# Seven-product tiles of a float32 attention and cosine feed-forward kernel: outputs in one run, the last product put off

## The chip, the cores and the metric

The kernel runs on one core of a Trainium2 chip. The metric is the device time of the whole program in microseconds (us). A core has TensorE (PE: matmuls; PEld is its loading of weights), VectorE (DVE), ScalarE (ACT), GpSimd (POOL) and SyncE (SP, whose queue issues the DMAs). Each engine works through its own instructions in the order of the program and waits for the others by semaphores.

## The reference

Chunked attention (64 positions to a chunk, 64 to a head) makes the 4608 x 512 matrix x, and a feed-forward layer with a cosine follows. All of it is float32.

```python
scores = scale * np.matmul(q_c, k_c.transpose(0, 1, 2, 4, 3))
scores = scores - np.max(scores, axis=-1, keepdims=True)
attn = np.exp(scores)
attn = attn / (np.sum(attn, axis=-1, keepdims=True) + 1e-09)
out = np.matmul(attn, v_c)
...
x = out.transpose(0, 2, 1, 3).reshape(B * S, H * D)   # 4608 x 512
h = x @ w_in                                          # 512 x 2048
g = h * np.cos(h)
return g @ w_out                                      # 2048 x 512
```

## The kernel before, in words

**Tiles.** The 4608 tokens are nine tiles of 512 (TOK). The 2048 hidden features are 16 chunks of 128 (fc), or eight pairs of chunks (k). Every float32 operand is split into a high part and a low rest, and a float32 product is three matmuls: high by high, high by low, low by high. Tiles 0 and 1 do the hidden layer directly (`hidden`, line 559). Tiles 2 to 8 do it by seven block products to a pair in place of eight (`pair`, line 804): A11, S3, S2, A12, A22, S1 and S4, each six matmuls of 256 columns, with sums of blocks of w_in that were made once, kept in HBM, and are streamed back two products at a time (`load_two`, line 733) into eight rooms in SBUF.

**A pair.** Two PSUM banks hold four halves: a and d in bank1, b and c in bank2. A11 goes to a, S3 to d. ScalarE copies a to b and d to the SBUF tile ds (line 839). S2 is added onto b, ScalarE copies b to c, A12 is added onto a, A22 onto c, S1 and at last S4 onto b. VectorE adds ds to c and b (`add`, line 842), which makes h2, the hidden values of the pair's second chunk; a and the final b are the two halves of the first chunk's.

**The cosine.** For each chunk g = h cos(h) is made in steps: `whole` (ScalarE, line 848: the number of turns as an integer), `turn` (VectorE, line 851: h less whole turns), `sine` (ScalarE, line 855), `times` (VectorE, line 858). The first chunk does this in halves of 256 columns, the second in one of 512. `high` (ScalarE, line 866, or VectorE, line 864, where exponentials stand in the queue) rounds g to its high part, and `low` (VectorE, line 870) makes the rest. Both are put into the next pair by the list `pair_before`.

**Output.** Each chunk of g gives four output parts (`projected_by_parts`, line 594), each three matmuls of 512 columns onto one of four PSUM banks acc0 to acc3, which add over the 16 chunks of a tile. The parts wait in the queue `due_parts`; `go(n)` (line 792) takes n of them. The last part of a bank puts `finish` (line 619) on the list `full`: a copy of the bank to SBUF (line 236) and a store. `go` empties `full` ahead of each part it takes. The next tile's first part begins anew in the same bank.

**Order.** From tile 2 on the order of every engine's instructions is written out by hand, and `kept` (line 224) holds it. A pair places its output parts at four points with the tuple `after`, normally (3, 0, 2, 3): three between S3 and S2, two between S1 and S4, three after S4. Where one tile's last parts are due (pair 1, with exponentials in the queue) it is (4, 0, 2, 2), with the copies of `finish` right behind the four.

**Attention of the next tile** runs between: `run_of_short` (line 941) puts a burst of 64 x 64 matmuls ahead of pair 0 (scores) and behind pair 5 (LAST_TURN; weighted values), using the two h banks and the two a banks of PSUM. After pair 0 the exponentials go to `exponentials_due`, two ScalarE instructions that pair 1 takes; Exp and Sin need different tables, which ScalarE loads in between. The sums, quotients and transpositions go to VectorE in the list `soon`, some at each of four places of a pair (`slots`); the next tile's x blocks are made in pairs 6 and 7 (`ahead`, `soon`).

PSUM has eight banks here: four acc, two h, two a. In the kernel before every pair uses the two h banks.

Of the kernel before, what the change touches and what calls it, by code (L numbers as in the profile page):

```python
# [21 lines left out]
P = 128  # L22
# [3 lines left out]
LAG = 3  # L26

PAD = 32

SHIFT = 28  # L30

# [166 lines left out]
def attention_then_cos_ffn(ctx: ExitStack, tc, qT, kT, v, w_in, w_out, out, wide):  # L198
# [65 lines left out]
    for fc in range(NFC):  # L264
        for name, n in (("in", NCC * P), ("out", DM)):
            if wide:
                raw = wts.tile([P, 4 * n + 2 * PAD], U16, name=f"w_{name}{fc}")
            else:
                raw = wts.tile([P, 2 * n + PAD], F32, name=f"w_{name}{fc}")
            w_raw[name, fc] = (raw, n)  # L270

    def load_weight(name, fc):
# [8 lines left out]
    def split_weight(name, fc, low):  # L281


        raw, n = w_raw.pop((name, fc))
        made = []

        def w():
            if not made:
                made.append(dec.tile([P, n], F32, name="w"))
            return made[0]  # L290

        nothing = lambda: None
        if not wide:
            pieces = [lambda: nc.gpsimd.tensor_copy(w(), raw[:, :n])] + [nothing] * 2
        else:

            both = raw.bitcast(U32)[:, : 2 * n].rearrange("p (n k) -> p n k", k=2)  # L300
            lower, upper = both[:, :, 0], both[:, :, 1]

            def joined():
                bits = w().bitcast(U32)
                kept(nc.vector.scalar_tensor_tensor(
                    bits, bits, 3, low, op0=ALU.logical_shift_left, op1=ALU.bitwise_or
                ))

            pieces = [
                lambda: kept(nc.scalar.activation(  # L310
                    w(), upper.bitcast(F32), AF.Prelu, scale=2.0 ** -(MORE // 8), alpha=-(2.0**32))),
                lambda: kept(nc.scalar.activation(low, lower, AF.Copy, scale=LOWEST)),
                joined,
            ]

        def high(by):
            o = SHIFT if name == "in" else 0
            parts = wts.tile([P, 2 * n + PAD], F32R, name=f"w_{name}{fc}")
# [251 lines left out]
    def activated(t, fc, h):  # L570


        g = gp.tile([P, TOK], F32, name="g", bufs=2)
# [20 lines left out]
    def projected_by_parts(s, sums_out):  # L594

        t, fc = order[s]
        first = s == 0 or order[s - 1][0] != t
        last = s == len(order) - 1 or order[s + 1][0] != t

        def part(sub):  # L600
            g_hi, g_lo = g_parts[t, fc]
            w_hi, w_lo = w_parts["out", fc]
            if first:
                acc[sub] = bank("acc", sub)
            o = acc[sub]
            ss = slice(sub * P, (sub + 1) * P)
            matmul(o, g_hi[:, ss], w_hi, start=first, stop=False)
            matmul(o, g_hi[:, ss], w_lo, start=False, stop=False)
            matmul(o, g_lo[:, ss], w_hi, start=False, stop=last)
            if last:  # L610
                sums_out.append(lambda by=None, sub=sub, o=o: finish(t, sub, o, fc == NFC - 1, by))

        return [lambda sub=sub: part(sub) for sub in range(NSUB)]

# [182 lines left out]
    def g_room():  # L797
# [3 lines left out]
        room = w_in_room(G_ROOM, F32R)[:, PAD:]  # L801
        return room[:, :TOK], room[:, TOK : 2 * TOK]

    def pair(t, k):
# [14 lines left out]

        b, c = bank2[:, :HALF], bank2[:, HALF:]  # L820
# [3 lines left out]
        def product(out, j, begin=False):  # L824
# [4 lines left out]
            for cc in range(2):  # L829
# [11 lines left out]
        def add(out, in_):  # L841
            kept(nc.vector.tensor_tensor(out, in_, ds, op=ALU.add))  # L842

        g1, g2 = (gp.tile([P, TOK], F32, name="g", bufs=2) for _ in range(2))
        first, second = slice(0, HALF), slice(HALF, TOK)

        def whole(g, h):
            kept(nc.scalar.activation(g.bitcast(I32), h, AF.Identity, bias=0.25, scale=0.5 / math.pi))  # L848

        def turn(g, h):  # L850
            kept(nc.vector.scalar_tensor_tensor(  # L851
                g, g.bitcast(I32), -2.0 * math.pi, h, op0=ALU.mult, op1=ALU.add))

        def sine(g):
            kept(nc.scalar.activation(g, g, AF.Sin, bias=0.5 * math.pi))  # L855

        def times(g, h):
            kept(nc.vector.tensor_tensor(g, h, g, op=ALU.mult))  # L858

        def high(g, fc):  # L860
            hi, lo = g_parts[t, fc] = g_room()

            if exponentials_due:
                kept(nc.vector.tensor_copy(hi, g))
            else:
                kept(nc.scalar.copy(out=hi, in_=g))  # L866

        def low(g, fc):
            hi, lo = g_parts[t, fc]
            kept(nc.vector.tensor_tensor(lo, g, hi.bitcast(F32), op=ALU.subtract))  # L870

        if behind:
            slots = [0, 1, 1, 2]
        elif k < LAST_TURN:
            slots = [1, 1, 1, 8]
        elif k == LAST_TURN:
            slots = [max(len(soon) - 2, 0), 1, 1, 0]
        elif k == LAST_TURN + 1:  # L880
            slots = [0, 1, 0, 3]
        else:
            slots = [0, 1, 1, len(soon)]
        ahead = deque(pieces.pop("ahead", ()))

        product(a, A11, begin=True)
# [36 lines left out]
        whole(g1[:, second], b)  # L923
        take(ahead, 1)
        turn(g1[:, second], b)
        sine(g1[:, second])
        turn(g2, h2)
        times(g1[:, second], b)
        sine(g2)
        times(g2, h2)  # L930

        pair_before.extend([
            lambda: high(g1, 2 * k), lambda: low(g1, 2 * k),
            lambda: high(g2, 2 * k + 1), lambda: low(g2, 2 * k + 1),
        ])
        take(soon, slots[3])
        s0 = STAGE + (t - 2) * NFC + 2 * k
        for s in (s0, s0 + 1):
            due_parts.extend(projected_by_parts(s, full))

    def run_of_short(t, scored):

# [447 lines left out]
```

## Time and profile before

| what | value |
| --- | --- |
| median of 3 runs | 833.36 us (832.65 to 833.37) |
| the profiled execution: span from first to last instruction | 831.5 us |
| mean granted TensorE clock | 0.995 |
| ScalarE's waits for TensorE ahead of line 839 | 138.2 us, 93 times |
| ScalarE's waits for VectorE ahead of line 855 | 132.1 us, 162 times |
| HBM read and written | 148.90 and 25.17 MB |

The median lies 1.9 us above the span of the profiled execution. The chain of waits follows the work back from the last instruction, at each step to what released it. Waits of an engine that is not on that chain cost nothing by themselves. In a row of the profile stand the engine, the line of the kernel, the operation, out<-in by the names of tiles, the shape, and the count; in a timeline the first two numbers are the start and the length in us, and a bracket at the end is the idle time ahead of it and what ended it.

### The profile page before, as it was taken

To read this page: it belongs to the slowest core of one execution; us is meant where nothing else is said; L and a number is where in the kernel's file an instruction comes from. 1 tells how busy PE (TensorE), PEld (TensorE's weight loads), DVE (VectorE), ACT (ScalarE), POOL (GpSimd) and SP (SyncE) were. 2 spreads that over 40 slices of the span, in tenths; PEclk is the share of its full clock that TensorE was granted. 3 is DMA by queue.
4 is the path that set the end of the run, shared out by engine and by line. 5 is a ranking of instruction groups with operands and counts; after the bars stand their busy time and mean duration, and the time that the engine had idled before them with its cause. 6 is when DMAs were issued, how large, how long until landed. Compare 5 with 4: busy or idle time off the path is not lost.

```text
span 831.5 us, 17325 instructions
## 1 busy us (share of the span) xinstructions
PE 817.8 (98%) x6800; PEld 717.9 (86%) x6800; DVE 648.0 (78%) x1222; ACT 466.2 (56%) x955; POOL 133.2 (16%) x127
## 2 busy tenths in 40 slices
PE   6999999999999999999999999999999999999998
PEld 5778888888888889988998899898988899899996
DVE  5889888877889688967897879878896889665443
ACT  4999865454554645463645464565446454644443
POOL 2455577586410000000000000000000000000000
PEclk8999999999999999999999999999999999999999
DMA  9991606485695766575757585676657565456521
GB/s 336 417 395 69 229 30 224 146 291 196 202 337 173 254 197 233 178 259 180 272 177 231 177 279 177 213 239 209 207 176 254 197 232 177 157 178 226 178 75 51
DMA packets 70034, 175.21 MB, mean 211 GB/s; under 512 B 6976, under 2 KB 21312, under 8 KB 69952
## 3 DMA queue, kind: packets, MB, share of 16 engines
q1 hardware_dynamic: 69952, 174.09, 61.6%
q8 instruction: 54, 0.88, 0.4%
q14 instruction: 28, 0.23, 0.1%
HBM read 148.90 MB, written 25.17 MB: 209 GB/s over the span
## 4 chain that ended last, share of the span: by engine, by line
PE 91%; DMA 6%; ACT 1%; DVE 1%; SPq 0%; issue 0%; DVEq 0%; ACTq 0%
PE acc L232 46%; PE h L232 44%; DMA w_out<-in_w_out_dram 4%; PE a L232 1%; DMA kt<-in_kT_dram 1%; DMA vt<-in_v_dram 1%; SPq L229 0%; DVE g L851 0%; ACT L446 0%; ACT L582 0%; PE a L475 0%; ACT w L310 0%; ACT x L543 0%; ACT e L446 0%; ACT g L855 0%
## 5 line engine op out<-in xcount | busy, mean ns | idle before, releaser
L232 PE MATMUL acc<-w_out,g_hi 128*128 128x512 f32 x928 | 289.7, 393 | 0.0
L232 PE MATMUL h<-x,w_in 128*128 128x256 f32 (+1 forms) x1728 | 269.0, 304 | 0.0
L232 PEld LDWEIGHTS h<-x,w_in 128*128 128x128 f32 x1728 | 244.1, 188 | 25.5 <-ACT h L839 2.2
L232 PEld LDWEIGHTS acc<-w_out,g_hi 128*128 128x128 f32 x928 | 164.6, 188 | 28.6
L232 PE MATMUL acc<-w_out,g_lo 128*128 128x512 f32 x464 | 181.2, 390 | 0.0
L855 ACT ACTIVATE g<-g 128x256 f32<-128x256 f32 x168 | 82.3, 490 | 132.1 <-DVE g L851 132.1
L232 PE MATMUL h<-w_in,w_in 128*128 128x256 f32 x1008 | 138.3, 281 | 0.5 <-ACT h L839 0.5
L232 PEld LDWEIGHTS h<-w_in,w_in 128*128 128x128 f32 x1008 | 129.3, 188 | 7.1 <-DVE w_in L842 2.2
L839 ACT COPY h<-h 128x256 f32<-128x256 f32 x112 | 40.0, 357 | 139.6 <-PE h L232 138.2
L232 PEld LDWEIGHTS acc<-w_out,g_lo 128*128 128x128 f32 x464 | 87.1, 188 | 19.2
L232 PE MATMUL acc<-w_out,w_in 128*128 128x512 f32 x336 | 86.0, 393 | 0.0
L842 DVE TENSOR_TENSOR w_in<-h,w_in 128x256 f32<-128x256 f32 x112 | 42.3, 419 | 43.6 <-ACT x L238 22.4
L870 DVE TENSOR_TENSOR g_lo<-g,g_hi 128x512 fp32r<-128x512 f32 x84 | 57.4, 686 | 23.5 <-ACT g_hi L866 22.1
L232 PEld LDWEIGHTS acc<-w_out,w_in 128*128 128x128 f32 x336 | 59.6, 188 | 10.3
L496 DVE STREAM_TRANSPOSE pts<-e 32x256 f32<-32x256 f32 x128 | 55.6, 435 | 1.9
L858 DVE TENSOR_TENSOR g<-w_in,g 128x512 f32<-128x512 f32 x56 | 39.1, 698 | 20.4 <-ACT g L855 20.4
L851 DVE SCALAR_TENSOR_TENSOR g<-g,h 128x256 f32<-128x256 int32 x112 | 46.4, 414 | 9.8 <-ACT g L848 9.0
L858 DVE TENSOR_TENSOR g<-h,g 128x256 f32<-128x256 f32 x112 | 46.9, 419 | 8.0 <-ACT g L855 6.8
L848 ACT ACTIVATE g<-h 128x256 int32<-128x256 f32 x112 | 43.0, 384 | 8.2 <-PE h L232 4.2
L866 ACT CAST g_hi<-g 128x512 fp32r<-128x512 f32 x72 | 44.9, 623 | 0.0
L496 DVE STREAM_TRANSPOSE e<-e 32x256 f32<-32x256 f32 x96 | 41.8, 436 | 1.7
L851 DVE SCALAR_TENSOR_TENSOR g<-g,w_in 128x512 f32<-128x512 int32 x56 | 38.8, 693 | 0.0
(116 smaller groups left out, 907.1 us busy)
## 6 DMA issues: line engine op xcount, KB each, us to landing
w_in<-combo SPq DMA_DIRECT2D x196, 512.0 KB, 4.0
combo<-w_in SPq DMA_DIRECT2D x56, 256.0 KB, 3.2
qt<-in_qT_dram SPq DMA_DIRECT2D x36, 256.0 KB, 5.4
kt<-in_kT_dram SPq DMA_DIRECT2D x36, 256.0 KB, 5.5
w_in<-in_w_in_dram SPq DMA_DIRECT2D x16, 512.0 KB, 9.8
w_out<-in_w_out_dram SPq DMA_DIRECT2D x16, 512.0 KB, 9.9
vt<-in_v_dram SPq DMA_DIRECT2D x22, 256.0 KB, 4.8
qt<-in_v_dram SPq DMA_DIRECT2D x12, 256.0 KB, 4.6
```

The source lines that it names most:

```text
L232: kept(nc.tensor.matmul(*args, **kw))
L496: kept(nc.vector.transpose(out=dst[o : o + BL, :, qb], in_=src[i : i + BL, :, kb]))
L839: kept(nc.scalar.copy(out=out, in_=in_))
L842: kept(nc.vector.tensor_tensor(out, in_, ds, op=ALU.add))
L848: kept(nc.scalar.activation(g.bitcast(I32), h, AF.Identity, bias=0.25, scale=0.5 / math.pi))
L851: kept(nc.vector.scalar_tensor_tensor(g, g.bitcast(I32), -2.0 * math.pi, h, op0=ALU.mult, op1=ALU.add))
L855: kept(nc.scalar.activation(g, g, AF.Sin, bias=0.5 * math.pi))
L858: kept(nc.vector.tensor_tensor(g, h, g, op=ALU.mult))
L866: kept(nc.scalar.copy(out=hi, in_=g))
L870: kept(nc.vector.tensor_tensor(lo, g, hi.bitcast(F32), op=ALU.subtract))
```

## The change

Four things, in tiles 2 to 8:

- The seventh product, S4, with the second half of the first chunk (whole, turn, sine, times) and that chunk's high and low (the list `rest`), is put off into the next pair, where S4 stands between S3 and S2. A pair without a next one in line (`whole_now`: pair 5 and pair 7 ahead of a burst, and the very last) does them itself. high(1) and low(1), those of the second chunk, now stand at the pair's own end.
- The output parts are taken in one place, behind S1: eight parts, 24 matmuls. A pair with none before it (pairs 0 and 6 of a tile, behind a burst) takes two parts between S3 and S2 and two at the end; a `whole_now` pair takes five, then S4, then three.
- Odd pairs use the two a banks, even pairs the two h banks.
- The second chunk of a pair now comes first in the order of output parts (`fc ^ 1`). Both exponentials are taken together behind copy(c, b). `finish` has no place of its own in a pair any more; `go` alone empties `full`. A third buffer for g takes the room of the padding behind the w_out tiles. A streamed room is loaded again after the later of its two reads.

```diff
+SPARE = {"in": PAD, "out": 0}
...
-    order += [(t, fc) for t in range(NT) if t != 1 for fc in range(0 if t else GROUP, NFC)]
+    order += [(0, fc) for fc in range(GROUP, NFC)]
+    order += [(t, fc ^ 1) for t in range(FAST, NT) for fc in range(NFC)]
...
-        behind = bool(exponentials_due)
-        if behind:
-            after = (4, 0, 2, 2)
-        elif len(due_parts) < 12:
-            after = (1, 0, 2, 1)
-        elif t == NT - 1 and k == NPAIR - 1:
-            after = (2, 1, 2, 0)
+        behind = lean[0] = bool(exponentials_due)
+        last = t == NT - 1 and k == NPAIR - 1
+        whole_now = last or t + 1 < NT and k == LAST_TURN or t + 2 < NT and k == NPAIR - 1
+        before = waiting.pop() if waiting else None
+        if k % 2:
+            bank1, bank2 = bank("a", 0), bank("a", 1)
         else:
-            after = (3, 0, 2, 3)
-        bank1, bank2 = (ps_h.tile([P, TOK], F32, name="h") for _ in range(2))
+            bank1, bank2 = (ps_h.tile([P, TOK], F32, name="h") for _ in range(2))
...
-            if n % 2:
+            reads[n // 2] = reads.get(n // 2, 0) + 1
+            if reads[n // 2] == 2:
                 load_two(fc)
...
+        rest = [
+            lambda: (product(b, S4), whole(0, b, second), turn(0, b, second)),
+            lambda: sine(0, second),
+            lambda: times(0, b, second),
+            lambda: high(0),
+            lambda: low(0),
+        ]
...
         product(a, A11, begin=True)
         product(d, S3)
         take(ahead, 1)
         copy(b, a)
         copy(ds, d)
         take(ahead, 1)
-        if not behind:
-            take(pair_before, 2)
-        go(after[0])
-        take(full, len(full))
-        if behind:
-            take(pair_before, len(pair_before))
-        take(exponentials_due, 1)
+        if before:
+            then(0)
+        else:
+            go(2)
         product(b, S2)
         copy(c, b)
-        take(exponentials_due, 1)
-        take(pair_before, len(pair_before))
-        take(ahead, 1)
+        take(exponentials_due, len(exponentials_due))
         product(a, A12)
-        product(c, A22)
-        whole(g1[:, first], a)
         take(ahead, 1)
         take(soon, slots[0])
-        go(after[1])
+        then(1)
+        then(2)
+        product(c, A22)
         product(b, S1)
+        whole(0, a, first)
+        take(ahead, 1)
+        turn(0, a, first)
         add(h2[:, first], c)
         add(h2[:, second], b)
-        turn(g1[:, first], a)
+        sine(0, first)
+        times(0, a, first)
+        then(3)
+        whole(1, h2)
+        take(ahead, 1)
+        then(4)
+        turn(1, h2)
+        sine(1)
         take(pair_after, len(pair_after))
         take(soon, slots[1])
-        sine(g1[:, first])
-        times(g1[:, first], a)
+        times(1, h2)
+        if before:
+            n = 8 if len(due_parts) >= 12 else 4
+        else:
+            n = 2
+        if last:
+            n = 4
+        elif whole_now:
+            n = 5
+        go(n)
+        if whole_now:
+            rest[0]()
+            go(8 if last else 3)
+            rest[1]()
+            rest[2]()
+        high(1)
         take(soon, slots[2])
-        go(after[2])
-        whole(g2, h2)
-        product(b, S4)
-        go(after[3])
...
+        low(1)
         take(soon, slots[3])
+        if whole_now:
+            pair_before.extend(rest[3:])
+        else:
+            waiting.append(rest)
```

`then(i)` runs the i-th entry of the list that the pair before left, if there is one. `low(i)` puts the four output parts of its chunk into `due_parts`.

More of the change, by code (lines that the diff above doesn't have):

```diff
@@ L317, in high @@
             o = SHIFT if name == "in" else 0
-            parts = wts.tile([P, 2 * n + PAD], F32R, name=f"w_{name}{fc}")
+            parts = wts.tile([P, 2 * n + SPARE[name]], F32R, name=f"w_{name}{fc}")
             hi, lo = parts[:, o : o + n], parts[:, o + n : o + 2 * n]
@@ L570, in activated @@
     def activated(t, fc, h):
-        g = gp.tile([P, TOK], F32, name="g", bufs=2)
+        g = gp.tile([P, TOK], F32, name="g")
         n = g.bitcast(I32)
@@ L842, in add @@
             kept(nc.vector.tensor_tensor(out, in_, ds, op=ALU.add))
-        g1, g2 = (gp.tile([P, TOK], F32, name="g", bufs=2) for _ in range(2))
+        g = {}
         first, second = slice(0, HALF), slice(HALF, TOK)
[L847 to L864, printed above, removed]
-            else:
[L866 to L870, printed above, removed]
+        def whole(i, h, part=slice(0, TOK)):
+            if i not in g:
+                g[i] = gp.tile([P, TOK], F32, name="g")
+            kept(nc.scalar.activation(g[i][:, part].bitcast(I32), h, AF.Identity, bias=0.25, scale=0.5 / math.pi))
@@ new lines, in turn, with sine, times, high @@
+        def turn(i, h, part=slice(0, TOK)):
+            o = g[i][:, part]
+            kept(nc.vector.scalar_tensor_tensor(
+                o, o.bitcast(I32), -2.0 * math.pi, h, op0=ALU.mult, op1=ALU.add))
+        def sine(i, part=slice(0, TOK)):
+            o = g[i][:, part]
+            kept(nc.scalar.activation(o, o, AF.Sin, bias=0.5 * math.pi))
+        def times(i, h, part=slice(0, TOK)):
+            o = g[i][:, part]
+            kept(nc.vector.tensor_tensor(o, h, o, op=ALU.mult))
+        def high(i):
+            hi, lo = g_parts[t, 2 * k + i] = g_room()
+            if lean[0]:
+                kept(nc.vector.tensor_copy(hi, g[i]))
+            else:
+                kept(nc.scalar.copy(out=hi, in_=g[i]))
@@ new lines, in low @@
+        def low(i):
+            hi, lo = g_parts[t, 2 * k + i]
+            kept(nc.vector.tensor_tensor(lo, g[i], hi.bitcast(F32), op=ALU.subtract))
+            s = STAGE + (t - FAST) * NFC + 2 * k + 1 - i
+            due_parts.extend(projected_by_parts(s, full))
+        rest = [
[5 more added lines that the diff above has]
+        ]
@@ L874, in pair, with then @@
+        def then(i):
+            if before:
+                before[i]()
         if behind:
@@ L882, in pair @@
         else:
-            slots = [0, 1, 1, len(soon)]
+            slots = [1, 1, 1, len(soon)]
         ahead = deque(pieces.pop("ahead", ()))
@@ L914, in pair @@
+        take(ahead, 1)
+        then(4)
+        turn(1, h2)
+        sine(1)
         take(pair_after, len(pair_after))
         take(soon, slots[1])
-        sine(g1[:, first])
-        times(g1[:, first], a)
-        take(soon, slots[2])
-        go(after[2])
-        whole(g2, h2)
-        product(b, S4)
-        go(after[3])
[L923 to L935, printed above, removed]
+        times(1, h2)
+        if before:
+            n = 8 if len(due_parts) >= 12 else 4
[11 more added lines that the diff above has]
+            rest[2]()
```

16 lines of the change are left out of this document (8 added, 8 removed).

## The prediction

> **What bounds the kernel now.** I read the page first, then the chain of waits.
>
> ```profile
> span 831.5 us, 17325 instructions
> PE 817.8 (98%) x6800; PEld 717.9 (86%) x6800; DVE 648.0 (78%) x1222; ACT 466.2 (56%) x955; POOL 133.2 (16%) x127
> ...
> PEclk8999999999999999999999999999999999999999
> ...
> PE 91%; DMA 6%; ACT 1%; DVE 1%; SPq 0%; issue 0%; DVEq 0%; ACTq 0%
> ```
>
> TensorE is on 91% of the chain that ended last. Nothing else can give much; anything that makes TensorE wait is paid in full. The chain in order of time has start, length and count of each piece:
>
> ```profile
> 196.70 2.72 PE acc L232 x12
> ...
> 320.90 2.82 PE h L232 x24
> ...
> 329.28 2.08 PE acc L232 x9
> 331.36 2.82 PE h L232 x24
> ```
>
> A product matmul (256 columns) takes 2.82/24 = 0.1175 us, an output matmul in an undisturbed stretch 2.72/12 = 0.2267. Two like pieces one pair apart start 331.36 - 320.90 = 10.46 us apart. A pair has 42 products and 24 output matmuls: 42 x 0.1175 + 24 x 0.2267 = 4.94 + 5.44 = 10.38. So only 0.08 us of a pair is lost. The nine output matmuls behind products take 2.08 where 9 x 0.2267 = 2.04: each change from products to outputs costs some 0.04.
>
> The change reorders all engines, so I need the hand-overs. Timelines of TensorE, ScalarE and VectorE, one fence each:
>
> ```profile
> 441.87 1.57 PE L232 MATMUL h<-w_in,w_in 128*128 128x256 f32 x12
> ```
> ```profile
> 466.60 0.86 PE L232 MATMUL acc<-w_out,w_in 128*128 128x512 f32 x3
> ```
> ```profile
> 441.37 0.36 ACT L839 COPY h<-h 128x256 f32<-128x256 f32 x1 [1.61 <-PE h L232]
> ```
> ```profile
> 464.95 0.62 ACT L866 CAST g_hi<-g 128x512 fp32r<-128x512 f32 x1
> 465.47 0.39 ACT L848 ACTIVATE g<-h 128x256 int32<-128x256 f32 x1
> ...
> 470.38 0.63 ACT L855 ACTIVATE g<-g 128x512 f32<-128x512 f32 x1 [0.18 <-DVE g L851]
> ```
> ```profile
> 466.80 0.76 DVE L842 TENSOR_TENSOR w_in<-h,w_in 128x256 f32<-128x256 f32 x2 [0.50 <-PE h L232]
> ...
> 471.05 0.69 DVE L858 TENSOR_TENSOR g<-w_in,g 128x512 f32<-128x512 f32 x1 [0.36 <-ACT g L855]
> ```
>
> From product S1's end (466.60, the next matmul starts) to VectorE: 0.20. From ScalarE's end (471.01) to VectorE: 0.04. From ScalarE's copy (ends 441.73) to the product that needs it: 0.14. Back to back on one engine, the next starts before the earlier ends: 465.47 is 0.52 behind 464.95, not 0.62. Further durations, from the groups by line and shape (mean ns is the second number behind the bar):
>
> ```profile
> L851 DVE SCALAR_TENSOR_TENSOR g<-g,w_in 128x512 f32<-128x512 int32 x56 | 38.8, 693 | 0.0
> L848 ACT ACTIVATE g<-w_in 128x512 int32<-128x512 f32 x56 | 34.5, 616 | 0.0
> L851 DVE SCALAR_TENSOR_TENSOR g<-g,h 128x256 f32<-128x256 int32 x112 | 46.4, 414 | 9.8 <-ACT g L848 9.0
> L858 DVE TENSOR_TENSOR g<-h,g 128x256 f32<-128x256 f32 x112 | 46.9, 419 | 8.0 <-ACT g L855 6.8
> L870 DVE TENSOR_TENSOR g_lo<-g,g_hi 128x512 fp32r<-128x512 f32 x84 | 57.4, 686 | 23.5 <-ACT g_hi L866 22.1
> L864 DVE CAST g_hi<-g 128x512 fp32r<-128x512 f32 x12 | 5.4, 449 | 0.0
> L702 ACT CAST w_in<-half 128x256 fp32r<-128x256 f32 x32 | 10.6, 407 | 0.0
> ```
>
> **Part 1: one run of 24.** TensorE's counts stay. A normal new pair is 42 products and one run of 24 with one change: 10.38 + 0.04 = 10.42, 0.04 saved. Over 56 pairs that is 2.3 us. Bounds: nothing, if the changes inside the pair cost nothing, and 56 x 0.08 = 4.5. Pairs that do S4 at once keep three changes, so I stay at 2.3.
>
> **Part 2: high(1) ahead of the next pair's copy.** The new program order of ScalarE ends a pair with high(1), the cast of the second chunk's g; the next pair's copy(b, a) is queued behind it, and product S2 waits for that copy. From the end of S1: 0.20, two adds 0.76, whole(1) 0.62, turn(1) 0.69, sine(1) 0.63, times(1) 0.69, five hand-overs 0.20, high(1) 0.52, copy 0.36, to TensorE 0.14: together 4.81 us. In a normal pair TensorE has 5.44 of outputs, 12 products (1.41) and the deferred S4 (0.71) in that time, 7.56, so 2.7 us to spare. But pairs 0 and 6 of a tile stand behind a burst, have no pair before them, and the code gives them go(2) at the end: 6 outputs. Then TensorE has 1.36 + 18 x 0.1175 = 3.48, and S2 waits 4.81 - 3.48 = 1.33 us. That happens at 0 to 1 and 6 to 7 in tiles 2 to 7: 12 x 1.33 = 16.0. In the first of them four casts of line 702 stand ahead of high(1); half is hidden behind times(1): 0.8 once. Bounds: 1.0 to 1.6 each, by how far instructions overlap.
>
> **Part 3: the border between two tiles falls inside pair 1's run.** Counting the queue of output parts (four to a chunk): eight are due at a pair's start, low(0) of the pair before adds four, go(8) takes eight. In pair 1 these are the four of the old tile's last chunk, then the first four of the new tile. The new tile's first part starts anew in bank acc0, so it must wait until VectorE has copied the old sum out (finish). In the kernel before this is arranged:
>
> ```profile
> 484.88 2.92 PE L232 MATMUL acc<-w_out,w_in 128*128 128x512 f32 x12
> ...
> 490.45 0.63 PE L232 MATMUL acc<-w_out,g_hi 128*128 128x512 f32 x2
> ```
> ```profile
> 485.77 0.69 DVE L236 COPY w<-acc 128x512 f32<-128x512 f32 x1
> ```
> ```profile
> 486.23 1.28 ACT L446 ACT_TABLE_LOAD   x1
> 487.53 1.06 ACT L446 ACTIVATE e<-e 128x1024 f32<-128x1024 f32 x1
> 488.53 0.36 ACT L839 COPY h<-h 128x256 f32<-128x256 f32 x1
> ...
> 490.16 1.28 ACT L855 ACT_TABLE_LOAD   x1
> 491.84 0.42 ACT L855 ACTIVATE g<-g 128x256 f32<-128x256 f32 x1 [0.40 <-DVE g L851]
> ```
>
> There the old tile's last 12 matmuls run from 484.88, VectorE copies from 485.77, and the new tile begins at 490.45, after 24 products. In the change the copies enter VectorE's queue behind times(1), and that chain now contains both exponentials and two table loads, since the deferred sine comes behind them on ScalarE. From S2's start in pair 1: S2 and hand-over 0.71 + 0.20; copy 0.36; table load 1.30 (486.23 to 487.53); exponentials 1.00 + 1.06; table load 1.30; deferred sine 0.42: 6.35. Then VectorE, in order: deferred times 0.42, turn 0.41, adds 0.76, times 0.42, high(0) 0.45, low(0) 0.69, turn(1) 0.69, together 3.84, less six overlaps of 0.08: 3.36. Then sine(1) 0.63, times(1) 0.69, copy out 0.60 (0.69 less the overlap), hand-overs 0.26. Sum 11.9. TensorE is there after 24 products and 12 outputs, 2.82 + 2.72 = 5.54. It waits 6.4 us, six times: 38.4. In the last tile nothing is exponentiated: 0.20 + 0.76 + 0.62 + 0.69 + 0.63 + 0.69 + 0.16 + 0.60 + 0.14 = 4.49 against 2.72, so 1.8. Queued behind the copies on VectorE are high(1) and low(1) of pair 1, whose readers come a pair later. Bounds: 5.6 (all overlap) to 6.9 (none).
>
> **Part 4: the clock.** Such a wait is long enough to ask about TensorE's granted clock. By stage (window, its length, busy times, clock):
>
> ```profile
> 12.00:15.00 3.00, 0.89 (x5) 0.65 (x6) 2.90 (x8) 1.45 (x4) 2.04 (x2) 0.96 1.05 406
> 15.00:22.00 7.00, 6.31 (x140) 5.18 (x139) 5.43 (x12) 5.34 (x13) 2.35 (x2) 0.53 1.05 405
> 22.00:30.00 8.00, 7.27 (x101) 6.12 (x93) 6.73 (x14) 6.85 (x15) 1.89 (x2) 1.00 1.03 415
> ```
> ```profile
> 61.04 1.16 PE L475 MATMUL a<-ident,e 128*128 128x128 f32 x8 [0.87 <-DVE x L546]
> ```
>
> TensorE was busy 0.89 of 3 us, and the next 7 us ran at 0.53, which is 7 x 0.47/0.5 = 6.6 us at half. A wait of 0.87 us at 61 us left full clock. So a wait of 6.4 us should bring half clock, part of it inside the wait itself. My estimate is 3.4 us of work at half speed, half of the slow stretch, losing 1.7 us: 6 x 1.7 = 10. Bounds: 0 (full clock) and 6.6/2 = 3.3 each, 20. The Trainium skill, "TensorE: Matmul & The Clock Gate", Part 1, says that one idle window of about 3.4 us halves the clock and about 3.4 us of work restores it; by that the loss would be the same 1.7 us, and it speaks against this change. The 1.33 us waits stay below what flipped the clock here.
>
> **Part 5: what costs nothing.** The third g buffer, from the padding of the w_out tiles, moves no work; the odd pairs' banks remove a wait that the chain does not show. A load of two products is issued after the later of its readers, S4 by some 5.44 + 1.41 = 6.9 us later on SyncE's queue:
>
> ```profile
> w_in<-combo SPq DMA_DIRECT2D x196, 512.0 KB, 4.0
> ```
>
> Eight rooms hold 16 products, 2.3 pairs or 24 us; 24 - 6.9 - 4.0 leaves 13. Without that cover each late load would stop TensorE for its lateness. The stores of finish stand in the same queue, behind them only loads for rooms not yet read. One stall of before goes, in tile 2's second pair, where the copy sat behind an exponential:
>
> ```profile
> 223.68 1.71 PE L232 MATMUL h<-w_in,w_in 128*128 128x256 f32 x12 [0.51 <-ACT h L839]
> ```
>
> 0.5 saved; what is late next there is Part 3's wait.
>
> **Sum.** 16.0 + 0.8 + 38.4 + 1.8 + 10 - 2.3 - 0.5 = +64.2 on the profiled 831.5: 895.7. The median of the runs, 833.36, is 1.9 above the span, so 897.6; I say 897.
>
> **Rivals.** (a) *All waits, clock stays full*: 897 - 10 = 887. For it: the clock stayed full through the later waits, 0.87 and 0.51 us; against it: these are a seventh of 6.4 and less. Chance 0.23. (b) *The border wait is short*, 1.8 us in every tile, because the copies get past the exponentials: 16.0 + 0.8 + 7 x 1.8 - 2.8 = +26.6, 860. Against it: before's own order on VectorE and ScalarE is the program's. Chance 0.09. (c) *Faster: TensorE never waits*, and only the fewer changes count: 833.4 - 2.8 = 830.6. It decides at one place: VectorE must end times(1) within 2.72 - 0.60 - 0.14 = 2.0 us of S1's end, or the border must fall between runs, if I miscounted the queue by four parts; and high(1) must be out of the way within 3.5 us. For it: normal pairs have 2.7 us to spare. Against it: the shortest chain I can build is 3.75 us. Chance 0.06. (d) The forecast, 0.62.
>
> **Numbers.** A measurement of this kernel can tell about 0.2%, 1.7 us, from no change. Forecast and (a) hold 0.85. Low end: (a) with overlaps at their best, 16 - 4 + 33.6 + 1.8 - 2.8 = +45, 878. High end: the clock's 20 in place of 10 and 3 of overlaps, 910. Within that 0.8; (b) and (c) are left out. Faster 0.06 from (c); 0.02 for small waits that eat (c)'s gain; slower 0.92.
>
> **What would show it.** Right: in tiles 2 to 7 TensorE's timeline has a gap over 5 us in pair 1 between two output matmuls, ended by VectorE's copy of acc (line 236); gaps of about 1.3 us ahead of S2 in pairs 1 and 7, ended by ScalarE's copy; the granted clock at 0.5 for a few us behind each long gap; normal pairs 10.42 apart. Wrong: output runs of 24 without a break at the border, or the copies of acc running ahead of times(1), or pairs 0 and 6 that hand over without a gap.

## The result, and the profile after

| | us |
| --- | --- |
| before, median of 5 runs | 833.24 (832.57 to 833.37) |
| after, median of 5 runs | 902.67 (901.74 to 903.96) |
| ratio after to before | 1.0837, 95% interval 1.0824 to 1.085 |
| span of the profiled execution after | 902.2 (831.5 before) |
| mean granted TensorE clock after | 0.974 (0.995 before) |

The kernel became 8.4% slower. The forecast was 897 with a range of 878 to 910. The profiled execution after took 903.96 us, 1.3 above the median, and the sums by kind below are of that one. The page of the profile after answers to the lines shown of before (the line numbers have moved: the matmul is line 233, the copies of acc are line 237, ScalarE's copy is line 845, the cosine's steps are lines 856 to 869, high is line 876 or 874, low line 880):

```profile
span 902.2 us, 17197 instructions
...
PE 837.6 (93%) x6800; PEld 729.7 (81%) x6800; DVE 648.4 (72%) x1222; ACT 469.9 (52%) x955; POOL 133.3 (15%) x127
...
PEclk8999999999899989999899989999999989999999
...
PE 79%; ACT 9%; DMA 6%; DVE 5%; issue 1%; SPq 0%; DVEq 0%; ACTq 0%
```

The matmuls are the same 6800, but TensorE's share of the chain that ended last fell from 91% to 79%; ScalarE and VectorE hold 14% of it, where they had 2%. The clock's row has an 8 in five slices in the body of the kernel, where before had none. The view of waits names what TensorE waited for (total, times, longest):

```profile
PE acc L233 <- DVE w L237: 31.8, 6, 6.1
PE a L233 <- ACT a L845: 13.2, 12, 1.5
PE acc L233 <- DVE x L638: 6.0, 1, 6.0
```

Six waits behind VectorE's copies of acc (one of them the 1.6 us of the last tile), one like them in tile 2, where VectorE adds the bank to an earlier sum at line 638, and twelve behind ScalarE's copy. Pair 1 of tile 5 on TensorE, with both kinds of wait (the row of 521.62 begins with product S2, the twelve from 524.56 are the old tile's last parts, and the new tile begins at 533.51):

```profile
521.62 1.67 PE L233 MATMUL a<-x,w_in 128*128 128x256 f32 x12 [1.11 <-ACT a L845]
...
524.56 2.89 PE L233 MATMUL acc<-w_out,w_in 128*128 128x512 f32 x12
533.51 1.22 PE L233 MATMUL acc<-w_out,g_hi 128*128 128x512 f32 x2 [6.05 <-DVE w L237]
```

Why the copy was late is seen on ScalarE, and then on VectorE, in the same stretch:

```profile
523.00 1.28 ACT L447 ACT_TABLE_LOAD   x1
524.29 2.01 ACT L447 ACTIVATE e<-e 128x1024 f32<-128x1024 f32 x2
526.32 1.28 ACT L865 ACT_TABLE_LOAD   x1
527.61 0.42 ACT L865 ACTIVATE g<-g 128x256 f32<-128x256 f32 x1
```
```profile
528.06 0.43 DVE L869 TENSOR_TENSOR g<-h,g 128x256 f32<-128x256 f32 x1 [5.46 <-ACT g L865]
...
531.39 0.68 DVE L457 TENSOR_REDUCE z<-e 128x8 f32<-128x512 f32 x1
532.16 0.69 DVE L869 TENSOR_TENSOR g<-w_in,g 128x512 f32<-128x512 f32 x1
532.77 0.68 DVE L237 COPY w<-acc 128x512 f32<-128x512 f32 x1
```

The deferred sine stands behind two table loads and both exponentials, 4.6 us; VectorE stands still for 5.46 us until it has the sine, and reaches the copy of acc at 532.77, though TensorE had filled that bank by 525.3 or so (the first three of the twelve from 524.56). The attention sum at 531.39 adds nothing: beside it ScalarE makes sine(1), from 531.50 for 0.63 us, and times(1) at 532.16 needs that.

The granted clock around this wait, in windows of the length in which the record changes it (start and end, length, PE busy with its count, PEld, VectorE, ScalarE and GpSimd, then the clock, and last the DMA engines' busy share and GB/s):

```profile
526.77:530.18 3.41, 0.69 (x4) 0.22 (x2) 2.09 (x7) 2.54 (x5) 0.00 (x0) 1.00 0.47 173
530.18:533.59 3.41, 0.08 (x1) 0.08 (x1) 3.31 (x6) 0.65 (x2) 0.00 (x0) 0.50 0.01 2
533.59:537.01 3.42, 3.42 (x8) 2.73 (x9) 3.42 (x7) 0.00 (x0) 0.00 (x0) 0.50 0.82 302
```

One window of little work is followed by one at half clock, and an empty one by another: half clock lasts from 530.18 to 537.01, of which TensorE works in the last 3.5 us. Behind the six border waits it works between 3.1 and 6.1 us at half clock, by where the windows' edges fall, and each costs about half of that, 1.5 to 2.9 us.

One more thing differs, and where nothing was changed: in tile 1. The chain in order of time (start, length, count), first of before, then of after:

```profile
128.76 2.72 PE acc L232 x12
131.48 2.72 PE h L232 x12
```
```profile
129.16 2.80 PE acc L233 x12
131.95 2.78 PE h L233 x12
134.74 2.76 PE acc L233 x12
```

The same code has runs of twelve of 2.80, 2.78 and 2.76 us where before has 2.72 in nearly all; every second run of the hidden layer (h) stays at 2.72 after, too.

**Where the 70.7 us of span went.** For each matmul of TensorE I took the time from its start to the next one's start, less 0.2267 us (512 columns) or 0.1174 (256); this is its excess. Summed by kind, after less before:

| part | us |
| --- | --- |
| waits ahead of S2 in pairs 1 and 7, twelve (1.18 to 1.62 each) | 15.1 |
| border waits, six (6.16 to 6.22) | 37.1 |
| the last tile's wait | 1.8 |
| before's one wait, gone | -0.7 |
| matmuls at half clock behind the border waits, 1.5 to 2.9 each | 12.0 |
| tiles 0 and 1: longer runs | 2.1 |
| tiles 2 to 8: output matmuls 1.0, product matmuls 2.5 | 3.5 |
| the rest (start of the program, transitions) | -0.2 |

### The profile page after: what moved, and what is told of

It reads as the page before. It is cut to its first block, busy times and chain, and to the rows that moved or that the text cites. A ratio compares the mean times of both kernels' runs of the same rounds, so it can differ in the third digit from the quotient of the medians.

```text
span 902.2 us, 17197 instructions
## 1 busy us (share of the span) xinstructions
PE 837.6 (93%) x6800; PEld 729.7 (81%) x6800; DVE 648.4 (72%) x1222; ACT 469.9 (52%) x955; POOL 133.3 (15%) x127
## 4 chain that ended last, share of the span: by engine, by line
PE 79%; ACT 9%; DMA 6%; DVE 5%; issue 1%; SPq 0%; DVEq 0%; ACTq 0%
PE acc L233 41%; PE h L233 23%; PE a L233 14%; DMA w_out<-in_w_out_dram 4%; ACT g L865 2%; DVE g L860 2%; DVE g L869 1%; ACT e L447 1%; ACT g L856 1%; DVE w_in L848 1%; ACT g_hi L876 1%; DMA kt<-in_kT_dram 1%; ACT x L239 1%; ACT L865 1%; ACT L447 1%
## 5 line engine op out<-in xcount | busy, mean ns | idle before, releaser
L233 PE MATMUL h<-x,w_in 128*128 128x256 f32 (+1 forms) x1056 | 183.4, 323 | 0.0
L233 PEld LDWEIGHTS h<-x,w_in 128*128 128x128 f32 x1056 | 158.4, 189 | 20.0 <-DVE g L585 0.3
L233 PE MATMUL a<-x,w_in 128*128 128x256 f32 x672 | 90.3, 283 | 13.2 <-ACT a L845 13.2
L233 PEld LDWEIGHTS a<-x,w_in 128*128 128x128 f32 x672 | 85.3, 188 | 18.2 <-ACT a L845 15.6
L233 PE MATMUL a<-w_in,w_in 128*128 128x256 f32 x504 | 69.1, 281 | 0.0
L233 PE MATMUL h<-w_in,w_in 128*128 128x256 f32 x504 | 68.8, 281 | 0.0
L233 PEld LDWEIGHTS a<-w_in,w_in 128*128 128x128 f32 x504 | 64.3, 188 | 1.0
L233 PEld LDWEIGHTS h<-w_in,w_in 128*128 128x128 f32 x504 | 63.5, 188 | 0.0
L869 DVE TENSOR_TENSOR g<-h,g 128x256 f32<-128x256 f32 x56 | 23.5, 419 | 36.1 <-ACT g L865 35.2
L860 DVE SCALAR_TENSOR_TENSOR g<-g,a 128x256 f32<-128x256 int32 x56 | 23.0, 411 | 35.3 <-ACT g L856 35.3
```

Of the source, the lines that this page charges most:

```text
L233: kept(nc.tensor.matmul(*args, **kw))
L860: kept(nc.vector.scalar_tensor_tensor(o, o.bitcast(I32), -2.0 * math.pi, h, op0=ALU.mult, op1=ALU.add))
L869: kept(nc.vector.tensor_tensor(o, h, o, op=ALU.mult))
```

## The experiments

Two theories stood at the outset. Mine: three causes that add up, VectorE's late copy of acc (because of the exponentials), high(1) ahead of ScalarE's copy, and, new since the result, the place of the w_out tiles without their spare words. The rival to the last: the runs of 24 themselves, or some contention with them, lengthen the matmuls.

**The exponentials behind sine(1)** (an edit of the kernel after):

```diff
-            slots = [0, 1, 1, 2]
+            slots = [0, 0, 0, 4]
...
         copy(c, b)
-        take(exponentials_due, len(exponentials_due))
         product(a, A12)
...
         sine(1)
+        take(exponentials_due, len(exponentials_due))
...
```

> The changed kernel with one edit: in pair 1 both exponentials stand behind sine(1), and the sums that need them behind low(1). My theory: the 6.2 us waits at the tile border are the length of the chain from S2 to VectorE's copy of acc, and 4.7 us of it are the exponentials and table loads. Then the border wait falls to about 2.2 us in tiles 2 to 7 (0.20 + 0.76 + deferred high and low 1.1 + turn 0.69 + sine 0.63 + times 0.69 + copy 0.60 + hand-overs, about 5.0, less 2.72), and the half clock behind it (2.0 us of loss each) is gone: 902.7 - 24 - 12 = 867. Rival: VectorE's own queue sets the wait and the exponentials only run beside it: over 5 us stays, 895 to 903. Second rival, on the clock: 2.2 us of idle TensorE halves the clock too: 879.

Measured: 878.81, ratio 1.0549 (1.0534 to 1.0563). The waits view:

```profile
PE a L233 <- ACT a L845: 13.2, 12, 1.5
PE acc L233 <- DVE w L237: 12.1, 6, 2.1
PE acc L233 <- DVE x L638: 3.5, 1, 3.5
```

So the exponentials made some 4 us of the border waits of tiles 3 to 7, and what is left, 2.1, comes from the copies' place behind times(1); the run that moves the border, below, tests that. In tile 2 (line 638) 3.5 is left: there VectorE's low, turn and times take 1.1 to 1.2 us in place of 0.69, in a stretch in which GpSimd sums blocks; why is not shown. The waits ahead of S2 are untouched, as a separate cause should leave them. But the time is at the rival's end of the expectation: the clock still fell behind five of the six remaining border waits. Two of them by windows, the first with a fall, the second without:

```profile
419.80:423.21 3.41, 1.31 (x7) 1.09 (x7) 2.71 (x6) 3.28 (x4) 0.00 (x0) 1.00 0.62 238
423.21:426.62 3.41, 3.41 (x11) 2.74 (x10) 3.38 (x7) 0.64 (x1) 0.00 (x0) 0.50 0.69 256
```
```profile
515.37:518.78 3.41, 1.72 (x7) 1.42 (x8) 3.07 (x6) 3.38 (x4) 0.00 (x0) 1.00 0.62 235
518.78:522.20 3.42, 3.42 (x25) 3.18 (x24) 3.39 (x7) 0.83 (x3) 0.00 (x0) 1.00 0.58 212
```

Both waits are 2.1 us. The first lies whole in one window, 2.1 of it idle, and the next window runs at half; the second is cut by a window's edge, 1.7 idle, and nothing happens. The five falls cost some 8 us.

**Pairs 0 and 6 leave high(1) and low(1) to the next pair**, behind its two copies (an edit of the kernel after):

```diff
         copy(ds, d)
+        take(held_over, len(held_over))
...
-        high(1)
-        take(soon, slots[2])
-        low(1)
+        if before or whole_now:
+            high(1)
+            take(soon, slots[2])
+            low(1)
+        else:
+            take(soon, slots[2])
+            held_over.extend((lambda: high(1), lambda: low(1)))
```

> The changed kernel with one edit: pairs 0 and 6 leave high(1) and low(1) to the next pair, behind its copies b and ds. My theory: the twelve waits of 1.2 to 1.6 us ahead of S2 come from copy(b, a) queued behind high(1), 15.1 us together; they go, the border wait of 6.2 stays as it is, because its chain starts at S2 and moves with it: 888. Rival: the six waits ahead of S2 in pair 1 and the border wait have the same chain upstream, so what is saved there comes back at the border: only the six of pair 7 go, 7.2 us: 895.

Measured: 892.38, ratio 1.071 (1.0693 to 1.0726).

```profile
PE acc L233 <- DVE w L237: 31.2, 6, 6.0
...
PE a L233 <- ACT a L846: 0.9, 1, 0.9
```

Of the twelve waits ahead of S2 one of 0.9 is left; the border waits stand as they were. The waits of tiles 2 to 8 sum to 39.4 in place of 54.0. Of these 14.6 us the medians show 10.3 and the spans of the two profiled executions 11.5 (902.2 to 890.7): 1.1 went to half clock (13.1) and some 2 to small delays of 0.1 to 0.2 us at restarts. The cause is shown; its price is 10 to 15 us.

**The spare words alone.** The kernel before, with nothing changed but the length of the w_out tiles:

```diff
+SPARE = {"in": PAD, "out": 0}
...
-                raw = wts.tile([P, 2 * n + PAD], F32, name=f"w_{name}{fc}")
+                raw = wts.tile([P, 2 * n + SPARE[name]], F32, name=f"w_{name}{fc}")
```

> The kernel before with one edit: the 32 spare words behind each w_out tile are taken out, nothing else. My theory from the two traces: in tiles 0 and 1, whose code is the same, output matmuls went from 227.0 to 231.3 ns apart and the stretch grew by 2.0 us, so it is the place of the tiles in SBUF that costs, about 5 us over the whole kernel: 838. Rival: the new order of tiles 2 to 8 costs it: 833.3, and the stretch of tiles 0 and 1 stays at 227.0.

Measured: 838.01, ratio 1.0061 (1.0048 to 1.0074), 4.9 us above before. Its chain in tile 1:

```profile
129.01 2.80 PE acc L233 x12
131.81 2.78 PE h L233 x12
```

These are the lengths of after, and tiles 0 and 1 lose the same 2.1 us. The rival falls: there is no run of 24 here.

**The spare words put back into the kernel after**, for fourteen of the sixteen w_out tiles (there is no room for more beside the third buffer of g); the two without lie last (where the tiles are made, `spare(name, fc)` stands in place of `SPARE[name]`):

```diff
+    def spare(name, fc):
+        return 0 if name == "out" and fc >= NFC - 2 else PAD
...
-        for name, n in (("in", NCC * P), ("out", DM)):
+        for name, n in (("in", NCC * P), ("out", DM))[:: -1 if fc == NFC - 1 else 1]:
...
```

> The changed kernel with the spare words back behind the w_out tiles 0 to 13 (there is no room for the last two), w_in 15 placed last, so that every w_out tile and all x and g tiles stand at the same place modulo 256 bytes as in the kernel before. My theory (place in SBUF): about 5 us less, 897.5, output matmuls of tiles 0 and 1 at 227.0 ns again. Rival (the order): 902.7.

Measured: 897.52, ratio 1.0779 (1.0765 to 1.0794), 5.2 us below after. The chain shows two like pairs side by side, first of after, then of this kernel (24 products of one pair as h x24, the run of 24 outputs, and the same 24 products of the next pair as a x24):

```profile
561.42 2.88 PE h L233 x24
564.30 5.55 PE acc L233 x24
...
571.99 2.86 PE a L233 x24
```
```profile
556.50 2.84 PE h L233 x24
559.34 5.47 PE acc L233 x24
...
566.91 2.84 PE a L233 x24
```

From x24 to x24 a pair takes 571.99 - 561.42 = 10.57 us after, and 10.41 with the spare words: the prediction's 10.42. Pairs 3 and 4 of every tile show the same: 10.52 to 10.57 after, 10.41 with the spare words, and 10.46 in nearly all before. So the run of 24 does save what was said of a normal pair, and the place of the tiles takes three times that.

**Which place?** From the code: a tile of w_in has 1056 words, 4224 bytes in a partition; one of w_out the same with its spare words and 4096 without. A chunk's two tiles then take 8448 = 33 x 256 bytes before and 8320 = 32.5 x 256 after: before, all w_out tiles begin at the same place modulo 256 (a multiple of 256, in the kernel as built), after, every second one begins 128 further, and so does every second tile of w_in. Two kernels without spare words separate this, by the order in which the tiles are laid out. In the first all w_out begin 128 past a multiple of 256, in the second at a multiple; w_in alternates in both, as in after:

```diff
...
-    for fc in range(NFC):
-        for name, n in (("in", NCC * P), ("out", DM)):
+    for name, fc in [("in", i) for i in range(NFC)] + [("out", i) for i in range(NFC)]:
+        for n in (NCC * P if name == "in" else DM,):
...
```

> The kernel before without the spare words, and the tiles placed in another order: every w_out tile begins at 128 modulo 256 bytes; w_in as in the run without spare words. My theory: an output matmul whose streamed operand begins at 128 modulo 256 takes 233.5 ns in place of 226.7 (the odd chunks in the run without spare words). Now all do: 840 to 843. Rival: it is not that place, but the alternation from chunk to chunk, or w_in: 833 or 838.

The second has the same edit with another order of the tiles:

```diff
...
+    for name, fc in [("in", 0)] + [("out", i) for i in range(NFC)] + [("in", i) for i in range(1, NFC)]:
...
```

> As the run before it, but every w_out tile begins at 0 modulo 256 bytes. My theory: outputs are back at 226.7 ns without any spare words; of the 5 us only what w_in's place costs the products is left, about 1.5: 834.5. Rival (the spare words themselves, or w_in): 838.

Measured: 839.97, ratio 1.0076 (1.0059 to 1.0092), and 836.28, ratio 1.0034 (1.0022 to 1.0046). The chains in tile 1, first with w_out at 128, then at 0:

```profile
135.45 2.80 PE acc L233 x12
```
```profile
129.30 2.73 PE acc L233 x12
132.02 2.79 PE h L233 x12
134.82 2.76 PE acc L233 x12
```

With w_out at 128 every run of outputs takes 2.80, 233.3 ns a matmul; at 0 they take 2.73 or 2.76, of which the 2.76 follow a longer run of the hidden layer. That the w_out tiles' place sets the outputs' pace is shown. The size was missed: 836.28 where 834.5 was expected, 2.9 us above before, with longer products (2.5 us of excess in tiles 2 to 8 where before has 1.0) and hidden matmuls. What is left is that w_in alternates (a tile of 4224 bytes is 16.5 x 256), where before has every one at 128 modulo 256. The kernel above with the spare words put back moved one w_in tile alone, that of chunk 15, to a multiple of 256; all other tiles stand as in before, modulo 256. Its chain at the end of tile 1 (the runs of the hidden layer are of chunks 14 and 15):

```profile
146.97 2.72 PE h L233 x12
...
152.42 2.79 PE h L233 x12
155.21 2.76 PE acc L233 x12
```

Of the undisturbed runs of the hidden layer only that of chunk 15 takes 2.79, and the outputs behind it 2.76, as for every second chunk with w_out at 0. So w_in's place sets the pace of the hidden layer. It makes 1.4 of the 2.9 us (tiles 0 and 1 with w_out at 0, against before); the products' 1.5 are likely of the same kind, but no run moved only what the products read.

**Exponentials behind sine(1), and the border at the end of pair 0.** Tile 2's pair 0 takes four parts at each of its two places, so that the old tile's last four parts end pair 0's run and the new tile's first part opens pair 1's:

```diff
+        take(full, len(full))
         if before:
...
-            go(2)
+            go(4 if (t, k) == (FAST, 0) else 2)
...
-            n = 8 if len(due_parts) >= 12 else 4
+            n = 8
         else:
-            n = 2
+            n = 4 if (t, k) == (FAST, 0) else 2
```

> The kernel of the run with the exponentials last, and besides: pair 0 of tile 2 takes four and four output parts, so that the queue stays four parts shorter for good and every tile border falls at the end of pair 0; the copies of acc are taken at the head of the next pair. My theory: the border wait is only the order (copies behind times(1) of the same pair), so it goes wholly in all seven tiles, with the half clock behind it: from 902.7, 37.1 + 1.8 of border waits and 12 of clock: 852. The twelve waits ahead of S2, 15.1 us, stay. Rival: the outputs taken a pair earlier now wait for low(0) of the pair before, and a new wait of 1 to 2 us per pair comes in place: 860 to 900.

Measured: 853.2, ratio 1.0236 (1.0221 to 1.0252).

```profile
PE a L233 <- ACT a L845: 11.7, 11, 1.1
```

No wait for a copy of acc is left, no window in the body of the kernel is at half, and the time is 49.5 below after: 37.1 + 1.8 of waits and 12.0 of clock make 50.9. Of the twelve waits ahead of S2 eleven stand nearly as they were (11.7, longest 1.1); the first, in tile 2, is gone, where four parts now end pair 0, and a new one of 0.5 comes in that tile's pair 2.

**The three mends together** (this one, the held-over high(1), and the spare words):

> All mends together: exponentials last, queue four parts shorter, high(1) and low(1) of pairs 0 and 6 left to the next pair, spare words back behind w_out. My theory: what is left is the change's own idea, one run of 24 output matmuls. By the traces so far its gain in run changes is 1.3 us, and before's one stall of 0.6 goes: 831.5 to 833.5, against 833.1 before. By the prediction's term it is 2.3 and 0.5: 830.3. Rival: small waits ahead of S2 (0.15 us each in the run with high(1) handed on) eat it: 834 to 838.

Measured: 842.05, ratio 1.01 (1.0085 to 1.0115). This missed both ranges: with the long waits gone, short ones are left of which before's order has fewer. TensorE and VectorE in pair 1 of a tile:

```profile
317.28 0.62 PE L233 MATMUL acc<-w_out,g_hi 128*128 128x512 f32 x2
...
318.34 0.73 PE L233 MATMUL acc<-w_out,g_hi 128*128 128x512 f32 x2 [0.23 <-DVE g_hi L879]
```
```profile
313.06 0.68 DVE L237 COPY w<-acc 128x512 f32<-128x512 f32 x1
...
317.88 0.41 DVE L879 CAST g_hi<-g 128x512 fp32r<-128x512 f32 x1
```

The run's fifth part, at 318.34, waits for a high that VectorE makes at 317.88, late behind the copies of acc and the deferred steps; and its first two matmuls take 0.73 where two others of the run take 0.62. Thirteen waits of 0.3 to 0.9 (5.3 us) and small ones of under 0.3 with their restarts (7.8, where before has 2.5) eat what the merged runs bring; the excess of the other output matmuls fell from 4.3 in before to 2.4.

**All that, with one exponential in pair 1 and one in pair 2, and all highs on ScalarE:**

```diff
-        behind = lean[0] = bool(exponentials_due)
+        behind = bool(exponentials_due)
...
-            slots = [0, 1, 1, 2]
+            slots = [0, 0, 0, 11 * (k - 1)]
         elif k < LAST_TURN:
-            slots = [1, 2, 1, 7]
+            slots = [1, 2, 1, 8]
...
         copy(c, b)
-        take(exponentials_due, len(exponentials_due))
+        take(held_over, len(held_over))
...
         sine(1)
+        take(exponentials_due, 1)
```

> As the run with all mends, but one exponential behind sine(1) in each of pairs 1 and 2, ScalarE makes all high parts, and the high(1) handed on stands behind copy(c, b). My theory: what kept the run with all mends at 842 were small waits, each with a restart of 0.1 us, for low and high parts that VectorE made late in pair 1 (about 1 us a tile), for copy(b, a) behind the exponentials in pair 2 (0.35) and for A22 behind high(1) in pairs 1 and 7 (0.27 each). They go, and the order is near its bound: 831 to 834 against 833.3. Rival: a run of 24 needs the same parts so much earlier that other waits take their place: 836 to 842.

Measured: 861.96, ratio 1.034 (1.0325 to 1.0354), a miss by 20 us and more. Six new waits of 3 to 4 us, one in pair 3 of each of tiles 2 to 7, 19.4 in all (20.1 with one of 0.75 in tile 2), with some 8 of half clock behind them. TensorE and VectorE there:

```profile
346.34 1.22 PE L233 MATMUL acc<-w_out,g_hi 128*128 128x512 f32 x2 [2.89 <-ACT g_hi L881]
```
```profile
337.55 2.46 DVE L461 TENSOR_REDUCE z<-e 128x8 f32<-128x512 f32 x4
...
343.66 0.42 DVE L865 SCALAR_TENSOR_TENSOR g<-g,h 128x256 f32<-128x256 int32 x1
```

Eleven attention steps (twelve instructions) stand in one place on VectorE, 337.55 to 343.66, ahead of the next pair's deferred turn; the sine, times and high behind it are late by as much. Two further kernels spread these eleven (the diff is against the kernel just shown, for the first of them): six in pair 2 (at most four in a place) and fourteen in each of pairs 3 and 4, or four and fifteen:

```diff
-            slots = [0, 0, 0, 11 * (k - 1)]
+            slots = [k - 1, k - 1, 0, 4 * (k - 1)]
         elif k < LAST_TURN:
-            slots = [1, 2, 1, 8]
+            slots = [2, 3, 1, 8]
```

> The kernel of e9 (862.0) with the eleven attention instructions that pair 2 put behind its low(1) on VectorE spread out: six in pair 2 (one at each of the first two places, four at the end), the others in pairs 3 and 4. Theory: e9's new wait of 3 to 4 us came from these eleven, 6.1 us of VectorE ahead of the next pair's deferred turn; with at most four in one place the six waits (20.1 us) and the half clock behind them (7.7) go, and the time is 833 to 836, waits below 2 us in all. Rival: the cause is the second exponential in pair 2 with its table loads, which delay the chain of high(0) whatever VectorE does; then a wait of 1 us or more stays in the run behind it and the time is 842 or above.

> As e10, with four attention instructions in pair 2 (one ahead of A22, three at the end) and fifteen in each of pairs 3 and 4. If what is left in e10 are delays by VectorE behind pair 2, this is 1 to 2 us faster than e10; if the fuller pairs 3 and 4 now make TensorE wait, it is slower than e10. Range 832 to 838; the prediction's savings and nothing else would give 830.6.

Measured: 852.56, ratio 1.023 (1.0213 to 1.0247), and 849.5, ratio 1.0196 (1.0181 to 1.0211). The waits of the first:

```profile
PE a L233 <- DVE e L501: 5.0, 6, 0.9
...
PE acc L233 <- ACT w_in L881: 3.3, 6, 0.6
```

The six long waits and the half clock are gone, so the eleven were their cause, and not the second exponential. The first time lies in the rival's range all the same, for a reason that neither theory had: the burst behind pair 5 now waits for transpositions that VectorE ends late (5.0), the output run of pair 4 for a high (3.3), and small waits add up to 10.0. The second is 3.1 us faster, but not for the reason in its expectation: the burst's waits for the same transpositions fall to 2.2, while those of pair 4's run for a high rise to 4.6. Its 849.5 is far above the 838 expected at most. No kernel of this order beat before; the fastest is the one at 842.05.

## Why the prediction was right, and where it was not

**Part 1, one run of 24: the gain was there, and small.** Normal pairs are 10.41 apart with the tiles in their old place; 10.42 was said. Over the kernel it is less than the 2.3 us: tiles 2 to 8 have 5.3 us of excess in their output and product matmuls before, 4.0 with the spare words back, so 1.3. In the kernel after, it is not to be seen at all, 10.52 to 10.57 a pair, for the reason under Part 5.

**Part 2, the hand-over: right.** Twelve waits at the places named, ended by ScalarE's copy, 15.1 us where 16.8 was said; holding high(1) back removed eleven of them. The extra 0.8 for the four casts of line 702 was 0.4: the first wait is 1.62, the others 1.18 to 1.28.

**Part 3, the border: right.** Six waits of 6.2 where 6.4 was worked out, 37.1 for 38.4, and 1.8 in the last tile as said. Taking the exponentials out of the chain left 2.1 us (3.5 in tile 2), and moving the border to a pair's end left none, so the two parts of the cause, the exponentials and the place behind times(1), are both shown.

**Part 4, the clock: right in kind, small in size.** 12.0 us for 10: the slow stretch is 6.8 us at every border wait, and TensorE works 6.1, 4.6, 3.9, 3.5, 3.1 and 3.1 us of it, 4.0 on the mean where 3.4 was estimated; at half speed that is 2.0 each in place of 1.7. How much of the stretch falls inside the wait goes by the windows' edges; the prediction took it as half. The place of the threshold was open in the prediction between 0.87 and 6.4; by the last section it is the idle time within one window that counts, and it lies near 2 us.

**Part 5, what costs nothing: the step that failed.** "The third g buffer, from the padding of the w_out tiles, moves no work" is true, and yet the padding had a price: 4.9 us by the kernel before without it, 5.2 by the kernel after with it. It was taken as room and not as place, and the term was put at nothing. The prediction looked for its cost at the queues and found none; a bound from the trace would have had to ask what else depends on where a tile lies. The rest of Part 5 held: the view of waits has no load and no bank of the odd pairs among TensorE's waits in tiles 2 to 8.

**The sum.** The forecast was 64.2 us, the span grew by 70.7. The difference of 6.5: waits -3.0, clock +2.0, before's stall -0.2, the tiles' place with the run of 24 +7.9 (from -2.3 to +5.6), the rest -0.2. The kernel with the spare words back measures 897.5 where 897 was forecast for after: apart from the tiles' place the errors cancel, -3.0 for the waits against +2.0 for the clock and +1.0 for the run of 24. That agreement is partly luck. The time after lies within the range, 5.7 us above the forecast, because the term that was missed is small beside the waits. Of the rivals, (a) falls with the clock at half in six places, (b) and (c) with the waits; the trace shows (d).

## What to carry to other kernels

When a change merges many short runs into a long one, count the queue at the borders first: what was spread over a pair (copies out of an accumulator, the last operand's rounding) now has one place, and every instruction ahead of that place on an in-order engine can become part of the wait. Room taken from padding moves all tiles behind it, so compare the pace of unchanged code (here tile 1) before explaining a change by its own mechanism. And in the last three kernels, moving VectorE's work to a place with slack on the average moved the wait with it; the place's own queue has to be read, instruction by instruction.

## What the runs showed of the hardware that was not expected

**The place of an operand in SBUF.** A matmul of 512 columns that streams a w_out tile runs at 0.2267 us when the tile begins at a multiple of 256 bytes (2.72 or 2.73 for twelve) and at 0.2333 (2.80/12) when it begins 128 bytes further; a run of twelve whose weights come from a w_in tile takes 2.72 with the tile at 128 and 2.79 with it at 0. No other places were tried, and why the place matters is not shown. The whole kernel took 838.01 us with every second w_out tile at 128, 839.97 with all and 836.28 with none, w_in alternating each time, against 833.2 with every tile at its old place.

**The clock follows windows of 3.413 us.** In the records every stretch at half clock in the body of a kernel is one or two such windows long and begins on one grid for the whole execution. In the profiled executions of before, of after and of all these kernels, behind the first 62 us, each window at full clock with TensorE idle for 2.08 us or more was followed by one at half (27 times), and none with 1.88 or less. So a wait of 2.1 us can cost more than itself, or nothing, by where the window's edge falls. The Trainium skill, "TensorE: Matmul & The Clock Gate", Part 1, has the free-running window of 3413 ns, and the grid agrees; it speaks of an idle window as what halves the clock, and here a window idle for three fifths was enough.

**A restart costs.** The first output matmul behind a wait takes some 0.1 us more (0.73 for two, against 0.62, in the rows above; 0.11 in each of 41 waits at full clock in these traces), so short waits cost a good deal more than the view of waits lists: the kernel at 842.05 has 7.8 us in delays of under 0.3.
